# One PSUM bank told to the list scheduler, mean-attention sums ranked before weight differences, and a lead-in put in another order

## The chip, the cores and the metric

The kernel runs on one NeuronCore of a Trainium2 chip. Its engines work side by side, each through its own queue in order: TensorE (PE) multiplies matrices and transposes, VectorE (DVE), ScalarE (ACT) and GpSimd (POOL) work element by element, SyncE (SP) issues most of the DMAs. They hand work to each other by semaphores. TensorE writes to PSUM, eight banks of 2 KB in each partition; ACT and DVE read from there. The metric is the device time of one execution in microseconds (us). 0.5% of this kernel's time is 7.86 us.

## The reference

Four batches of eight heads over 576 positions with 64 channels go through two attentions, whose sum is the input of a mixture of eight experts.

```python
# mean attention: groups of 4 positions averaged, 144 x 144 softmax attention, result repeated 4 times
q_d = q.reshape(B, H, Sd, factor, D).mean(axis=3)         # k_d, v_d alike
out_up = np.repeat(sm_attn(q_d, k_d, v_d), factor, axis=2)
# local attention: each position looks at |distance| < 4, so at most 7 neighbours
mask = np.abs(pos[:, None] - pos[None, :]) < factor
...
attn_out = out_up + out_local                              # becomes x: 2304 tokens x 512
# experts
logits = x @ w_gate
P = np.exp(logits - logits.max())
for _ in range(8):                                         # Sinkhorn over all tokens and experts
    P /= P.sum(1, keepdims=True) + 1e-09
    P /= P.sum(0, keepdims=True) + 1e-09
    P *= N / E
for e in range(E):
    out += P[:, e:e+1] * (np.maximum(x @ w1[e], 0) @ w2[e])   # w1[e] 512x1024, w2[e] 1024x512
```

## The kernel before

**Products.** Every fp32 product of the experts is three passes of TensorE over rounded parts: high x high, high x low, low x high. So each weight piece is converted twice: its high half by ACT (`w1h`, `w2h`), its low half as a difference by POOL, sometimes DVE (`w1l`, `w2l`, L1994 and L1998). A unit is one 128-wide slice of one expert's hidden layer over a group of tokens: 12 matmuls give `psh` (L1842), ACT makes `hh` from it by ReLU (L1906), DVE the rest `hl` (L1909), and three matmuls for each tile of tokens (L1876 to L1878) add to `psy`.

**Stages.** (1) The lead-in computes the attention of the first 256 tokens, so that the experts can start. Its steps (`k_part`, `q_part`, `s_part`, ...) are put in order by a planner (`Plan.schedule`) from the hand-written list `LEAD` (L2138) and estimated lengths. While TensorE has nothing to do there, dummy matmuls (L2586, 128 x 400) run. (2) From then to about 560 us the units are mixed with the rest of the attention. Here generators ("threads") yield the engine they need next and the time from which they are ready, and `sched` (L2023 on) always steps the thread with the earliest estimated start, ties by `RANK` (L2019). The clocks of that estimate, one for each engine, are the program's, not the chip's: they decide only in which order instructions are written into the queues. (3) Two more plans, Mid and Final, work through the remaining tokens with a scheme that saves multiplications (`psm`, L588 to L783). The change is to stages 1 and 2.

**The bank.** One PSUM bank, `psd`, is used by several threads in turn. `d_gen` (mean attention) transposes and sums the query groups into it on TensorE (L1448), ACT copies them out as `qz` (L1457), TensorE computes scores into another bank (`pss`, L1507), later transposes the probabilities through `psd` (L1540; ACT copies out `pt`, L1545) and writes the result (L1569; ACT copies out `od`, L1578). `g_gen` (gate logits) uses it with a DVE reader. Besides, 112 columns of the same bank, `scp`, hold the weights of the local attention: DVE writes them (L1214, `psd<-sc,mx`) and reads them in four products (L1228, `prod<-lw,psd`). The framework orders any two instructions that touch the bank on different engines in the order in which they are written. The scheduler before knows two numbers of this: `psd_r`, the end of the last DVE product, for which a TensorE writer (engine name `"ped"`) waits, and `psd_w`, the end of the last TensorE write, for which a DVE product waits. ACT's copies and DVE's write of `scp` ask for neither.

**Other threads that the change touches.** `p_gen` (`"p"` in `RANK`) forms the sums for the mean attention on POOL (`dr<-lw`, `dr<-lq`, L1350). `paced` spreads DMAs for the coming part over the units. `raw_next` issues the weight pieces on SP (L1002, L1007), as buffers come free.

## Time and profile before

| | us |
|---|---|
| median of 3 runs | 1571.87 (1570.53 to 1576.81) |
| profiled execution | 1573.13 |
| its span, first to last instruction | 1571.4 |
| TensorE busy | 1555.8 |
| DVE busy | 1335.6 |
| POOL busy | 1072.3 |
| ACT busy | 823.9 |

The profiled execution took 1573.13 us, of which 1.7 us lie outside the span; it is 1.26 us above the median. TensorE is busy for 99% of the span, at a mean granted clock of 0.999 of full speed. Since a TensorE instruction counts as busy also while it is slow, single places are read from the timeline: start of one, start of the next. In a row of the timeline the part in brackets is the time for which the engine stood idle before the instruction, and what released it.

### The profile page before, as it was taken

What the parts mean: (1) busy time and instruction counts of PE and PEld (TensorE: products, weight loads), DVE (VectorE), ACT (ScalarE), POOL (GpSimd) and SP (SyncE); (2) the same over time, 40 slices, a digit from 0 to 9 for tenths busy, and PEclk for the clock granted to TensorE, in tenths of its full rate; (3) what the DMA queues carried; (4) which work ended last, traced back from release to release, by engine and by line L of the source; (5) the groups of instructions that cost most, each with busy time, mean ns of one, the idle gap of its engine ahead of it and who ended that gap; (6) DMA issues with size and microseconds to landing.
All of it is one profiled execution on the core that took longest, in us unless ns stands there. A gap on an engine that the chain in (4) does not pass through costs nothing.

```text
span 1571.4 us, 24610 instructions
## 1 busy us (share of the span) xinstructions
PE 1555.8 (99%) x8243; PEld 1315.7 (84%) x8243; DVE 1335.6 (85%) x1875; ACT 823.9 (52%) x1748; POOL 1072.3 (68%) x1022
## 2 busy tenths in 40 slices
PE   8999999999999999999999999999999999999998
PEld 7888888889887888889999988888888888888887
DVE  6778888888988696478999797999989999999987
ACT  5653555465554524365555445555555555555553
POOL 8687566769755600287777548878777777878872
PEclk9999999999999999999999999999999999999999
DMA  9877767769763645423332372212121222121102
GB/s 206 222 206 193 166 163 186 183 186 240 212 164 105 195 138 180 145 62 104 97 119 61 120 213 78 74 54 75 58 70 58 75 60 75 57 68 54 48 14 54
DMA packets 232187, 190.06 MB, mean 121 GB/s; under 512 B 28732, under 2 KB 190460, under 8 KB 232060
## 3 DMA queue, kind: packets, MB, share of 16 engines
q1 hardware_dynamic: 225068, 176.36, 41.1%
q10 hardware_dynamic: 6992, 12.13, 2.3%
q8 instruction: 64, 1.05, 0.3%
q14 instruction: 63, 0.52, 0.1%
HBM read 166.25 MB, written 22.18 MB: 120 GB/s over the span
## 4 chain that ended last, share of the span: by engine, by line
PE 83%; DMA 4%; POOL 4%; issue 4%; DVE 3%; SPq 1%; ACT 1%; ACTq 0%; POOLq 0%; DVEq 0%
PE psm L588 26%; PE psm L600 19%; PE psh L1842 14%; PE psm L783 7%; PE psy L1876 5%; PE psy L1878 4%; PE psy L1877 4%; DMA r<-in_moe_w_dram 2%; POOL w2l L1998 2%; POOL w1l L1998 2%; PE pss L1507 1%; DMA lw<-in_k_dram 1%; DVE acc L794 0%; DMA dr<-in_v_dram 0%; DMA lw<-in_v_dram 0%
## 5 line engine op out<-in xcount | busy, mean ns | idle before, releaser
L571 POOL TENSOR_TENSOR o<-r,o 128x512 fp32r<-128x512 f32 x126 | 166.0, 1317 | 88.0 <-ACT o L567 87.5
L1998 POOL TENSOR_TENSOR w1l<-r,w1h 128x512 fp32r<-128x512 f32 x114 | 155.7, 1366 | 89.4 <-ACT w1h L1975 76.9
L1998 POOL TENSOR_TENSOR w2l<-r,w2h 128x512 fp32r<-128x512 f32 x115 | 158.0, 1374 | 23.4 <-ACT w2h L1975 18.2
L588 PE MATMUL psm<-th,o 128*128 128x512 f32 x512 | 173.0, 389 | 0.0
L1876 PE MATMUL psy<-w2h,hh 128*128 128x512 f32 x408 | 165.0, 404 | 0.3 <-ACT hh L1906 0.3
L622 DVE TENSOR_TENSOR acc<-psm,acc 128x512 f32<-128x512 f32 x216 | 144.7, 682 | 20.9 <-PE psm L600 20.7
L1878 PE MATMUL psy<-w2h,hl 128*128 128x512 f32 x408 | 159.7, 391 | 0.6 <-DVE hl L1909 0.6
L1877 PE MATMUL psy<-w2l,hh 128*128 128x512 f32 x408 | 159.6, 391 | 0.0
L600 PE MATMUL psm<-hx,o 128*128 128x512 f32 x564 | 151.1, 389 | 0.0
L1906 ACT ACTIVATE hh<-psh 128x512 fp32r<-128x512 f32 (+1 forms) x136 | 67.5, 496 | 149.6 <-PE psh L1842 141.3
L571 POOL TENSOR_TENSOR o<-xh,o 128x256 fp32r<-128x256 f32 x132 | 111.2, 849 | 50.2 <-ACT o L567 42.4
L1909 DVE SCALAR_TENSOR_TENSOR hl<-psh,hh 128x512 fp32r<-128x512 f32 (+1 forms) x136 | 76.1, 561 | 69.6 <-ACT hh L1906 68.8
L588 PE MATMUL psm<-xh,o 128*128 128x512 f32 x384 | 131.2, 389 | 0.3 <-DVE hl L2094 0.3
L1842 PE MATMUL psh<-xhs,w1h 128*128 128x256 f32 (+1 forms) x384 | 125.9, 328 | 0.6 <-ACT xhs L2253 0.6
L1975 ACT ACTIVATE w2h<-r 128x512 fp32r<-128x512 f32 x134 | 84.2, 629 | 78.9 <-PE psy L1878 28.5
L600 PEld LDWEIGHTS psm<-hx,o 128*128 128x128 f32 x564 | 105.8, 188 | 22.0
L1842 PE MATMUL psh<-xls,w1h 128*128 128x256 f32 (+1 forms) x384 | 122.8, 320 | 0.5 <-DVE xls L2518 0.5
L1842 PE MATMUL psh<-xhs,w1l 128*128 128x256 f32 (+1 forms) x384 | 122.8, 320 | 0.0
L567 ACT ACTIVATE o<-r 128x512 fp32r<-128x512 f32 x139 | 87.3, 628 | 55.5 <-PE psm L600 35.6
L588 PEld LDWEIGHTS psm<-th,o 128*128 128x128 f32 x512 | 96.1, 188 | 20.1
L1252 DVE TENSOR_REDUCE lo<-prod 128x256 f32<-128x1792 f32 x32 | 109.6, 3425 | 0.1
L571 POOL TENSOR_TENSOR xh<-xh,xh 128x256 fp32r<-128x256 f32 x32 | 24.8, 782 | 116.0 <-ACT xh L567 115.8
(379 smaller groups left out, 4556.8 us busy)
## 6 DMA issues: line engine op xcount, KB each, us to landing
r<-in_moe_w_dram SPq DMA_DIRECT2D x367, 256.0 KB
xh<-in_moe_w_dram SPq DMA_DIRECT2D x108, 128.0 KB
spill<-sp ACTq DMA_DIRECT2D x40, 256.0 KB
s<-spill SPq DMA_DIRECT2D x40, 256.0 KB
xl<-in_moe_w_dram SPq DMA_DIRECT2D x68, 128.0 KB
g<-gd SPq DMA_DIRECT2D x16, 256.0 KB
sums<-dr SPq DMA_DIRECT2D x36, 64.0 KB
r2x<-in_moe_w_dram SPq DMA_DIRECT2D x9, 256.0 KB
```

What stands on the lines that cost most here:

```text
L567: self.nc.scalar.activation(out=self.get(v)["h"], in_=self.w_view(l, r, ps), func=AF.Copy)
L571: (self.nc.gpsimd if pool else self.nc.vector).tensor_tensor(out=o["l"], in0=self.w_view(l, r, ps), in1=o["h"].bitcast(F32), op=ALU.subtract)
L588: self.nc.tensor.matmul(out=ps, lhsT=wt[:, k], rhs=xt[:, k], start=start and n == 0, stop=n == 5, skip_group_check=not start,)
L600: self.nc.tensor.matmul(out=ps, lhsT=wt[:, a, 128 * m:128 * m + 128], rhs=ht, start=start and n == 0, stop=n == 5, skip_group_check=not start,
L622: self.nc.vector.tensor_tensor(out=self.get(o[0]), in0=self.get(a[0]), in1=self.get(b[0]), op=op)
L783: self.nc.tensor.matmul(out=ps, lhsT=self.at_tile(ht, t), rhs=wt[:, a], start=start and n + t % 2 == 0, stop=n == 5, skip_group_check=not ...
L1252: nc.vector.tensor_reduce(out=ot[:, :, h % 2], in_=pr.rearrange("p r w d -> p r d w"), axis=AX.X, op=ALU.add,)
L1842: nc.tensor.matmul(out=ps, lhsT=w[:, kk], rhs=x[:, kk], start=(kk == 0 and j == 0), stop=(kk == 3 and j == 2),)
L1876: nc.tensor.matmul(out=ye[z], lhsT=hh[:, ts], rhs=h2, start=(f2 == 0), stop=False)
L1877: nc.tensor.matmul(out=ye[z], lhsT=hh[:, ts], rhs=l2, start=False, stop=False)
L1878: nc.tensor.matmul(out=ye[z], lhsT=hl[:, ts], rhs=h2, start=False, stop=(f2 == NF - 1))
L1998: nc.gpsimd.tensor_tensor(out=l, in0=r, in1=h.bitcast(F32), op=ALU.subtract)
```

## The change

It has five parts.

1. **The bank in the scheduler.** Instead of `psd_r` and `psd_w` there is one time for each of TensorE, ACT and DVE (`psd_e`). Who uses the bank starts, in the estimate, no earlier than the last use by another engine. `"ped"`, `"actd"` and `"dved"` mark such steps for TensorE, ACT and DVE. The normalization of the local weights is cut in two, so that DVE can do something else between the reciprocal and the write of `scp`.
2. **Ranks and margins.** `"p"` goes from 3.5 to 2.5, which puts it before the weight differences that are not urgent (3). TensorE steps that are not units get an estimated margin of 0.4 instead of 0.15 us. The key and query windows come two parts a unit instead of one.
3. **Start of the lead-in.** 13 dummy matmuls instead of 17, and TensorE's planned start at 5.9 instead of 6.4.
4. **Its order.** `w1` (the second unit's weights) stands later in `LEAD`; its conversions wait for the first `xhs`. The mask operations of POOL (`mk...`) are planned to be due only at the end and are taken to be twice as long.
5. **The first unit.** The six matmuls of each half are sorted so that the two with `xls` come last. The clocks with which stage 2 begins are set about 1 to 2.4 us later.

```diff
-    psd_r, psd_w = [0.0], [0.0]
+    psd_e = {"pe": 0.0, "act": 0.0, "dve": 0.0}
+    def psd_after(e):
+        return max(t for z, t in psd_e.items() if z != e)
+    def on_psd(e, t):
+        psd_e[e] = t
+        return t
...
-            yield t + HOP, "dve", 0.9, True
+            yield t + HOP, "dve", 0.6, True
             nc.vector.tensor_reduce(out=mx, in_=sc3, axis=AX.X, op=ALU.add)
             nc.vector.tensor_scalar(out=mx, in0=mx, scalar1=EPS, scalar2=None, op0=ALU.add)
             nc.vector.reciprocal(out=mx, in_=mx)
+            dve(112, t)
+            dve(16, lock=True)
+            t = dve(128)
+            yield t, "dved", 0.3, True
             nc.vector.tensor_tensor(
                 out=scp.rearrange("p h r w -> p (h r) w"), in0=sc3,
...
-            dve(112, lock=True)
+            on_psd("dve", dve(112, t, psd_after("dve"), lock=True))
...
-                yield max(tv[h], psd_w[0]), "dve", 2.05, False
+                yield tv[h], "dved", 2.05, False
...
-            yield from paced(u + 1, l_win_parts(u + 1, k, l_k))
+            yield from paced(u + 1, l_win_parts(u + 1, k, l_k), 2)
...
-            t = psd_w[0] = d_done[b, hf] = pe(1.6, t0, psd_r[0])
+            t = d_done[b, hf] = on_psd("pe", pe(1.6, t0, psd_after("pe")))
             d_taken.add((b, hf))
-            yield t + HOP, "act", 0.0, False
+            yield t + HOP, "actd", 0.0, False
             for i in range(2):
                 o = slice(64 * i, 64 * i + 64)
                 nc.scalar.activation(out=qz[o, :, i, Q0:], in_=ps[o], func=AF.Copy, scale=scale / (R * R))
-                t_qk = act(2 * Q1, t)
+                t_qk = on_psd("act", act(2 * Q1, t, psd_after("act")))
...
-                for kk in part:
-                    for j, (w, x) in enumerate(((h1, vh), (h1, vl), (l1, vh))):
+                terms = [(kk, w, x) for kk in part for w, x in ((h1, vh), (h1, vl), (l1, vh))]
+                if not n:
+                    terms.sort(key=lambda z: z[2] is vl)
...
-    RANK = {"h": 0, "raw": 0, ... "p": 3.5, ... "m": 2, "v": 2}
+    RANK = {"h": 0, "raw": 0, ... "p": 2.5, ... "m": 2, "v": 2}
...
-                en = "pe" if t.eng == "ped" else t.eng
-                st = max(t.ready, clk[en])
+                en = t.eng[:-1] if t.eng in ("ped", "actd", "dved") else t.eng
+                st = max(t.ready, clk[en], psd_after(en) if en != t.eng else 0.0)
...
-                    st = max(t.ready + 0.15, clk["pe"], psd_r[0] if t.eng == "ped" else 0.0)
+                    st = max(t.ready + 0.4, st)
...
-        LEAD = "k0 q0 ... v0 t0 s2 w1 v2 ct0 ... o3 p3 x1 w0".split()
+        LEAD = "k0 q0 ... v0 t0 s2 v2 ct0 ... o3 p3 w1 x1 w0".split()
...
+            after = [x_h[0]] if n else []
...
-                op("act", f"wh{n}{j}", [v_r[n]], [a], lambda h=h, j=j: cp("act", h, r[j]), 512)
+                op("act", f"wh{n}{j}", [v_r[n]] + after, [a], lambda h=h, j=j: cp("act", h, r[j]), 512)
...
-                op("pool", f"mk{len(P.ops)}", [], [v], emit, 56)
+                op("pool", f"mk{len(P.ops)}", [], [v], emit, 120)
...
-        work = P.schedule({"act": 7.1, "dve": 5.1, "pool": 5.1, "pe": 6.4})
+        for o in P.ops:
+            if o.name.startswith("mk"):
+                o.by = P.seq[-1]
+        work = P.schedule({"act": 7.1, "dve": 5.1, "pool": 5.1, "pe": 5.9})
...
-                for _ in range(int((o.start - t - 0.1) / 0.18) if t else 17):
+                for _ in range(int((o.start - t - 0.1) / 0.18) if t else 13):
...
-        begin = {"pe": 27.0, "dve": 29.5, "act": 29.2, "pool": 29.6, "port": 29.6, "sp": 27.5, "dma": 32.0}
-        land = {"lk": 28.0, "lq": 29.0, 2: (31.0, 32.0)}
+        begin = {"pe": 28.2, "dve": 30.2, "act": 29.8, "pool": 32.0, "port": 32.0, "sp": 28.5, "dma": 33.5}
+        land = {"lk": 30.5, "lq": 33.2, 2: (34.5, 35.3)}
```

The same replacement as in `d_gen`'s first copy stands at every other use of the bank. What the new numbers do to the queues is shown at three places. The first is ACT's queue around the copy of the second half of the first batch's queries (`qz_107<-psd`), with what each instruction waits for. Before:

```order
L1578 ACTIVATE od<-psd 128x2x80 [waits PE_49]
L1975 ACTIVATE w2h<-r_1027 128x512 [waits DMAHW6_49,Pool_49]
L1906 ACTIVATE hh<-psh 128x256 [waits DVE_49,PE_49]
L1951 DMA spill<-sp 128x512 [waits Activation_49]
L1457 ACTIVATE qz_107<-psd 64x2x80 [waits DVE_49,PE_49]
L1457 ACTIVATE qz_107<-psd 64x2x80
```

After:

```order
L1585 ACTIVATE od<-psd 128x2x80 [waits PE_49]
L1984 ACTIVATE w2h<-r_1020 128x512 [waits DMAHW6_49,Pool_49]
L1915 ACTIVATE hh<-psh 128x256 [waits DVE_49,PE_49]
L1464 ACTIVATE qz_107<-psd 64x2x80 [waits PE_49]
L1464 ACTIVATE qz_107<-psd 64x2x80
```

The copy no longer waits for DVE, only for TensorE. On DVE the same place reads as follows before, where `psd<-sc,mx` and `prod<-lw,psd` are the bank's users:

```order
L1212 TENSOR_SCALAR mx<-mx 128x16
L1213 RECIPROCAL mx<-mx 128x16
L1214 TENSOR_TENSOR psd<-sc,mx 128x112
L1909 SCALAR_TENSOR_TENSOR hl<-psh,hh 128x256
L1228 TENSOR_TENSOR prod<-lw,psd 128x1792
L1514 MEMSET st 80x6
```

And after:

```order
L1220 TENSOR_SCALAR mx<-mx 128x16
L1221 RECIPROCAL mx<-mx 128x16
L1918 SCALAR_TENSOR_TENSOR hl<-psh,hh 128x256
L1226 TENSOR_TENSOR psd<-sc,mx 128x112
L1237 TENSOR_TENSOR prod<-lw,psd 128x1792
L1521 MEMSET st 80x6
```

`hl` now stands ahead of the write into the bank, which itself waits for ACT's copy. The second place is SP's queue after the lead-in: weight pieces (`r_...`), the queries of the next mean attention (`dr`) and the values of the next local window (`lw`). Before:

```order
L1002 DMA r_579<-in_moe_w_dram 128x4x128
L1007 DMA r_581<-in_moe_w_dram 128x512
L1002 DMA r_657<-in_moe_w_dram 128x4x128
L1325 DMA dr<-in_q_dram 80x4x256 x2
L1104 DMA lw<-in_v_dram 32x2x512
...
L1104 DMA lw<-in_v_dram 32x2x384
L1007 DMA r_716<-in_moe_w_dram 128x512
```

After:

```order
L1010 DMA r_575<-in_moe_w_dram 128x4x128
L1015 DMA r_577<-in_moe_w_dram 128x512
L1332 DMA dr<-in_q_dram 80x4x256 x2
L1112 DMA lw<-in_v_dram 32x2x512
...
L1112 DMA lw<-in_v_dram 32x2x384
L1010 DMA r_684<-in_moe_w_dram 128x4x128
L1015 DMA r_703<-in_moe_w_dram 128x512
```

The first weight piece of the sixth unit (`r_657` before, `r_684` after) has gone from ahead of the ten attention loads to behind them. The third place is POOL's queue at the end of the lead-in, where `dv` is the last sum of the first mean attention, `w1l` and `w2l` the first two units' weight differences and `wg` the gate's. Before:

```order
L2343 TENSOR_TENSOR dv<-vsum 72x2x2x64
L2536 TENSOR_TENSOR w1l<-r_196,w1h 128x512
L2536 TENSOR_TENSOR w2l<-r_198,w2h 128x512
L2536 TENSOR_TENSOR w1l<-r_200,w1h 128x512
L2536 TENSOR_TENSOR w2l<-r_202,w2h 128x512
L2213 TENSOR_TENSOR wg<-wgr,wg 128x4x8
L1998 TENSOR_TENSOR w1l<-r_319,w1h 128x512
```

After:

```order
L2352 TENSOR_TENSOR dv<-vsum 72x2x2x64
L2546 TENSOR_TENSOR w1l<-r_196,w1h 128x512
L2546 TENSOR_TENSOR w2l<-r_198,w2h 128x512
L2546 TENSOR_TENSOR w1l<-r_200,w1h 128x512
L2546 TENSOR_TENSOR w2l<-r_202,w2h 128x512
L2561 TENSOR_SCALAR ef<-ef 32x56
L2577 TENSOR_SCALAR mask<-ef 128x56
L2579 TENSOR_TENSOR mask<-mask 128x56
L2580 TENSOR_SCALAR mask<-mask 128x56
L2222 TENSOR_TENSOR wg<-wgr,wg 128x4x8
L2007 TENSOR_TENSOR w1l<-r_311,w1h 128x512
```

Four mask operations, which stood before the sums of the values, now stand between the weight differences and `wg`. Over the whole program two weight differences go from DVE to POOL, and four first additions to the output go through a copy by ACT; the matmuls of the units and of the attention are the same, in a slightly different mixture.

## Rows read from the trace of the kernel before

**Rows 1.** The page's line of busy times, by engine.

```profile
PE 1555.8 (99%) x8243; PEld 1315.7 (84%) x8243; DVE 1335.6 (85%) x1875; ACT 823.9 (52%) x1748; POOL 1072.3 (68%) x1022
```

**Rows 2.** The page's chain that ended last, by engine.

```profile
PE 83%; DMA 4%; POOL 4%; issue 4%; DVE 3%; SPq 1%; ACT 1%; ACTq 0%; POOLq 0%; DVEq 0%
```

**Rows 3.** Waits of TensorE: waiting line, what for, us, times, longest.

```profile
PE pss L1507 <- ACT qz L1457: 2.3, 1, 2.3
PE psg L1647 <- DVE xl L1630: 1.0, 1, 1.0
...
PE psd L1723 <- DVE stmp L1712: 0.7, 1, 0.7
```

**Rows 4.** Timeline, 66 to 72 us: start, us, instruction, [idle before].

```profile
66.33 1.33 PE L1448 MATMUL psd<-ident,dr 80*64 80x80 f32 x32
...
67.76 1.08 DVE L1214 TENSOR_TENSOR psd<-sc,mx 128x112 f32<-128x112 f32 x1 [1.22 <-PE psd L1448]
...
69.09 2.00 DVE L1228 TENSOR_TENSOR prod<-lw,psd 128x1792 f32<-128x1792 f32 x1
...
71.19 0.30 ACT L1457 ACTIVATE qz<-psd 64x160 f32<-64x160 f32 x1 [4.36 <-DVE st L1514]
...
71.54 1.08 PE L1507 MATMUL pss<-kz,qz 128*80 128x144 f32 x4 [2.27 <-ACT qz L1457]
```

**Rows 5.** Stretches: busy by engine, granted clock, DMA share, GB/s.

```profile
28.00:50.00 22.00, 20.07 (x178) 16.82 (x175) 15.69 (x16) 10.81 (x25) 14.47 (x13) 1.00 0.96 244
...
72.00:74.00 2.00, 2.00 (x11) 2.00 (x11) 0.45 (x1) 1.81 (x6) 1.46 (x2) 0.50 0.36 133
74.00:76.00 2.00, 2.00 (x10) 1.85 (x10) 0.62 (x3) 0.72 (x3) 1.05 (x1) 0.67 0.42 125
```

**Rows 6.** Timeline, 45 to 49 us: the same steps for the first half.

```profile
46.70 0.62 ACT L1457 ACTIVATE qz<-psd 64x160 f32<-64x160 f32 x2 [0.88 <-PE psd L1448]
...
48.09 0.65 PE L1507 MATMUL pss<-kz,qz 128*80 128x144 f32 x4
48.49 0.38 PE L1842 MATMUL psh<-xhs,w1h 128*128 128x256 f32 x1
```

**Rows 7.** Timeline of the lead-in, TensorE and one row of DVE.

```profile
1.33 5.95 PE L2586 MATMUL psd<-wz 128*128 128x400 f32 x17 [1.33 <-DVE wz L2131]
...
5.83 0.69 DVE L2342 TENSOR_TENSOR gs<-dr 72x512 f32<-72x512 f32 x1 [0.62 <-DMA dr<-in_k_dram]
...
7.21 1.15 PE L2249 MATMUL leadz<-ident,dr 64*64 64x64 f32 x32
8.29 1.97 PE L2249 MATMUL leady<-ident,lq 128*64 128x128 f32 x32
...
31.38 0.39 PE L1842 MATMUL psh<-xhs,w1h 128*128 128x256 f32 x1 [0.64 <-ACT xhs L2253]
32.10 0.38 PE L1842 MATMUL psh<-xls,w1h 128*128 128x256 f32 x1 [0.34 <-DVE xls L2518]
...
34.23 0.28 PE L1647 MATMUL psg<-xhs,wg 128*16 128x256 f32 x1
```

**Rows 8.** Timeline of the lead-in, POOL.

```profile
17.80 0.36 POOL L2567 TENSOR_SCALAR mask<-ef 128x56 f32<-128x56 f32 x1
...
27.58 1.28 POOL L2536 TENSOR_TENSOR w1l<-r,w1h 128x512 fp32r<-128x512 f32 x1
...
32.53 0.25 POOL L2213 TENSOR_TENSOR wg<-wgr,wg 128x32 fp32r<-128x32 f32 x1
```

**Rows 9.** Timeline of SP's queue, 33 to 45 us.

```profile
36.73 0.37 SPq L1002 DMA_DIRECT2D r<-in_moe_w_dram  x1
37.15 1.01 SPq L1325 DMA_DIRECT2D dr<-in_q_dram  x2
38.27 5.99 SPq L1104 DMA_DIRECT2D lw<-in_v_dram  x8
```

**Rows 10.** Waits of POOL: the sums of the mean attention.

```profile
POOL dr L1350 <- DMA lq<-in_q_dram: 13.9, 6, 4.0
```

More of the change, by code (lines that the diff above doesn't have):

```diff
@@ L1232, in pv_prod @@
                 if eng is nc.vector:
[L1233 to L1235 removed]
+                    return on_psd("dve", dve(R * W * D, tv[h], *deps, psd_after("dve")))
                 return pool(R * W * D, tv[h], *deps)
@@ L1276, in ld_gen @@
             yield t + HOP, "sp", 0.0, False
-            yield from paced(u + 1, l_win_parts(u + 1, k, l_k))
+            yield from paced(u + 1, l_win_parts(u + 1, k, l_k), 2)
             yield t + HOP, "sp", 0.0, False
-            yield from paced(u + 1, l_q_parts(u + 1))
+            yield from paced(u + 1, l_q_parts(u + 1), 2)
             while u not in v_free or u >= U1 and (u, 2) not in s_read:
@@ L1477, in d_gen @@
                         )
-                t = psd_w[0] = pe(0.3, t0, t1, psd_r[0])
+                t = on_psd("pe", pe(0.3, t0, t1, psd_after("pe")))
                 if p == 1:
@@ L1481, in d_gen @@
                     d_done[b, hf] = t
-                yield t + HOP, "act", 0.0, False
+                yield t + HOP, "actd", 0.0, False
                 for i in range(2):
@@ L1542, in r_gen @@
                     )
-                t2 = psd_w[0] = pe(0.1 * nb, t, psd_r[0])
-                yield t2 + HOP, "act", 0.0, False
+                t2 = on_psd("pe", pe(0.1 * nb, t, psd_after("pe")))
+                yield t2 + HOP, "actd", 0.0, False
                 nc.scalar.activation(out=pt[:, p, kh], in_=ps2.rearrange("a i t -> a (i t)"), func=AF.Copy)
-                t_pt[0] = act(nq * nb, t2)
+                t_pt[0] = on_psd("act", act(nq * nb, t2, psd_after("act")))
                 sd.free(t_pt[0])
@@ L1573, in d_gen @@
                     )
-        t = psd_w[0] = pe(8 * 0.15, t_pt[0], psd_r[0])
-        yield t + HOP, "act", 0.0, False
+        t = on_psd("pe", pe(8 * 0.15, t_pt[0], psd_after("pe")))
+        yield t + HOP, "actd", 0.0, False
         if b and hf == 0:
@@ L1580, in d_gen @@
         )
-        od_t[b, hf] = act(288, t)
+        od_t[b, hf] = on_psd("act", act(288, t, psd_after("act")))
         sd.free(od_t[b, hf])
@@ L1664, in g_gen @@
             )
-        t = psd_w[0] = pe(0.07 * nt, t, psd_r[0])
-        yield t + HOP, "dve", 0.3, False
+        t = on_psd("pe", pe(0.07 * nt, t, psd_after("pe")))
+        yield t + HOP, "dved", 0.3, False
         nc.vector.tensor_reduce(
@@ L1670, in g_gen @@
         )
-        t = dve(2 * E * nt, t)
+        t = on_psd("dve", dve(2 * E * nt, t, psd_after("dve")))
         sd.free(t)
@@ L1839, in m_gen @@
                     ps = ps_h.tile([128, nt], F32, tag="h", name="psh")
-                for kk in part:
-                    for j, (w, x) in enumerate(((h1, vh), (h1, vl), (l1, vh))):
-                        nc.tensor.matmul(
-                            out=ps, lhsT=w[:, kk], rhs=x[:, kk],
-                            start=(kk == 0 and j == 0), stop=(kk == 3 and j == 2),
-                        )
+                terms = [(kk, w, x) for kk in part for w, x in ((h1, vh), (h1, vl), (l1, vh))]
+                if not n:
+                    terms.sort(key=lambda z: z[2] is vl)
+                for z, (kk, w, x) in enumerate(terms):
+                    nc.tensor.matmul(
+                        out=ps, lhsT=w[:, kk], rhs=x[:, kk],
+                        start=(part[0] == 0 and z == 0), stop=(part[0] == 2 and z == len(terms) - 1),
+                    )
                 t = pe(mm_t(nt, 6), deps)
@@ L2047, in sched @@
                     rank = 4 if nm == "l" else 5
-                    if hq and t.eng == "dve" and t.dur > 1.0:
+                    if hq and en == "dve" and t.dur > 1.0:
                         n, _, nt, te = hq[0]
@@ L2054, in sched @@
                     rank = RANK.get(nm, 5)
-                if t.lock and t.eng == "dve" and t.dur <= 2.1 and st - max(t.ready, clk["dve"]) > PATIENCE:
+                if t.lock and en == "dve" and t.dur <= 2.1 and st - max(t.ready, clk["dve"]) > PATIENCE:
                     rank = 0.4
@@ L2266, in attention_moe_kernel @@
         v_q = there("q", 6.9)
-        v_k = [there(f"k{n}", (6.0, 9.3, 9.9, 10.8)[n]) for n in range(NP)]
+        v_k = [there(f"k{n}", (5.8, 9.3, 9.9, 10.8)[n]) for n in range(NP)]
         v_w = there("vw", 13.0)
@@ L2475, in ct_part @@
             st["pt", hf] = pt.rearrange("a (p k i t) -> a p k i t", p=2, k=2, i=2), x
-        o_at, v_s = {}, {}
+        o_at, v_s, x_h = {}, {}, {}
         def o_part(n):
@@ L2515, in x_part @@
             sx = lp.rearrange("p (z t) -> p z t", z=2)
-            xw = new(f"xh{hf}")[0]
+            xw = x_h[hf] = new(f"xh{hf}")[0]
             op("act", f"xh{hf}", [b], [xw], lambda: cp("act", xh[0][:, z, 0:256], sx), 512)
@@ L2600, in attention_moe_kernel @@
         for n in w_unit:
-            w_ready[n] = (25.7, 27.0) if n == 0 else (28.3, 29.6)
+            w_ready[n] = (27.0, 28.3) if n == 0 else (30.0, 31.3)
             raw_rel.extend(w_ready[n])
```

14 lines of the change are left out of this document (4 added, 10 removed).

## The prediction

> **What bounds the kernel now.** I read the page's busy line first: TensorE is busy for 1555.8 of 1571.4 us, the next engine, DVE, for 1335.6 [rows 1]. The chain of waits agrees: 83% of it is TensorE [rows 2]. No matmul of the units goes away, so the change can only give back time in which TensorE stood idle or ran at the lower clock, and can only lose by making it idle more. The list of TensorE's waits says how much there is: one wait of 2.3 us of the scores `pss` for ACT's copy `qz`, one of 1.0 for `xl` and one of 0.7 for `stmp`, and little else in stage 2 [rows 3]. The timeline shows what stands behind the long one [rows 4], the stretches what the clock did after it [rows 5], and the lead-in is read from its own timeline [rows 7, 8].
>
> **Part 1, the bank: the long stall.** Before, TensorE's 32 transposes into the bank end at 66.33 + 1.33 = 67.66. Then DVE takes the bank: its write of the local weights at 67.76 (1.08), one `hl`, and the product at 69.09 (2.00). ACT's copy may start only behind the product, at 71.19, after 4.36 us of idling, and `pss` starts at 71.54 after TensorE has idled 2.27 [rows 4]. In the new order ACT's copy waits for TensorE alone, and DVE's write waits for the copy. The two copies take 0.62 together where nothing comes between, as in the first half of the same queries, where `pss` followed without an idle time [rows 6]. So they run from about 67.8 to 68.4, and `pss` has its input 0.9 us before TensorE is through with its matmuls (71.54 - 2.27 = 69.27). The idle time goes: -2.3. DVE loses about 0.6 for this (its write starts at 68.4 instead of 67.76), less the `hl` that now stands ahead of it; DVE has no follower that TensorE waits for at this place, because `hl` has been moved ahead. If that cover is gone, the price is those 0.6.
>
> After the stall the granted clock is 0.50 from 72 to 74 us and 0.67 from 74 to 76, and TensorE was busy all the while [rows 5]. 0.50 is 1.2 of 2.4 GHz. Lost: 2 x 0.50 + 2 x 0.33 = 1.7 us. The stretch follows directly on the one long idle time in this stage, so with that gone I take it to go as well: -1.7. The bounds are 0 and -1.7. Part 1 together: **-4.0**.
>
> **Part 1, the other places.** The scheduler now holds an ACT copy or a DVE write back, in its estimate, while another engine has the bank, and writes other instructions ahead of it. Elsewhere in the order some copies by ACT (`pt`) now come behind a 2.0 us product of DVE that they preceded before. ACT's queue is in order, so `hh` of a unit stands behind such a copy; TensorE waits for it if the wait is longer than the other unit's matmuls last. The trace of before does not show these places. From below: each could win a stall back, but there are only the waits of 1.0 and 0.7 [rows 3], so at best -1.7 in all. From above: one bad place costs what the one in the trace did, 2.3 and the slow stretch, 4.0 [rows 3, 5]. Both waits in the list are of DVE being late at another moment than the bank's, so a reshuffled DVE queue meets them or not, about evenly: **-0.9**, with the ends -1.7 and +4.0.
>
> **Part 2, ranks and margins.** The sums on POOL (`dr`) come some units earlier, ahead of weight differences. In before they have waited 13.9 us in six places for the query loads, at most 4.0 [rows 10]. A sum in front of a difference now makes the difference wait for that load. POOL is busy for 1072 of 1571 us [rows 1], so a difference that is late by one such wait can be made up, and the wait meets TensorE only if the weights were prepared less than 4.0 ahead. I take 0, since no wait of TensorE for a difference is in the list of before [rows 3], and keep +4.0 as the end: one such wait in full. The larger margin only moves TensorE's small steps behind a unit: 0.
>
> **Parts 3 to 5, the lead-in.** 17 dummies last 5.95 us, 0.35 each, the lower level for 400 columns [rows 7]. Four fewer free TensorE 1.4 us earlier, at about 5.85. The first keys are there: DVE's first sum of them starts at 5.83, released by their DMA [rows 7]. So the first transposes start at 5.85 instead of 7.21, -1.36, unless they now run at the lower level: 32 of them take 1.15 at full speed [rows 7], at most twice that, so they end between 1.36 and 0.2 earlier. What follows is a chain over four engines, and POOL's part is relieved too, as the four mask operations (0.36 for the one shown [rows 8], some 1.6 in all) leave its path ahead of the values' sums. The first unit idles 0.64 and 0.34 for its second `xhs` and `xls` [rows 7]; sorted, it meets the second of these later, -0.3. Gain at the second unit: 1.7 at best.
>
> Part of it is lost again within 15 us. First, the mask operations now stand ahead of `wg`. POOL's four differences take from 27.58 to 32.53 [rows 8], 4.95 us; begun 1.5 us earlier, plus 1.6 for the masks, `wg` is done at about 32.9, and the gate's matmuls, at 34.23 before [rows 7], would want it at 32.5: +0.5. Second, the sixth unit's first weights. Before, SP issued them at 36.73, then the queries from 37.15 and the values from 38.27 for 5.99 us [rows 9]. Now they come behind all ten loads, of 1.54 MB. SP no longer waits until 36.73, so the loads start at about 33.7. With two pieces in flight, the loads and the piece itself, 2.3 MB at the 244 GB/s of this stage [rows 5] take 9.4 us: landing at 43.1 at the earliest, and up to 47 if more is in flight. The sixth unit started at 48.49 [rows 6] and now wants its weights at about 47, after a conversion and a difference that take 1.3 more. So the loss lies between 0 and 1.3, I take +0.5. The lead-in nets -1.7 + 0.5 + 0.5 = **-0.7**, with the ends -1.7 and, if the first transposes run slowly and both losses come in full, +1.0.
>
> The moment at which the clock rises could itself move. The Trainium skill ("TensorE: Matmul & The Clock Gate", Part 1, "What's actually happening") says that the default state is the throttled one and that activity releases it. In the trace the dummies ran at the lower level up to about 7 us and the first transposes at full speed, so row and rule agree on the order. The same page says that the moment varies from run to run, by half a microsecond; by that rule the -1.36 would be -1.36 plus or minus 0.5, which no row here can show.
>
> **The sum.** -4.0 - 0.9 - 0.7 = -5.6 us against the profiled execution: 1573.13 - 5.6 = 1567.5. That execution lies 1.26 above the median of the runs. Against the median the forecast is 1571.87 - 5.6 = **1566.3**. A change of 0.5%, 7.86 us, is about what a measurement of this kernel can tell from none: faster means below 1564.0, slower above 1579.7.
>
> **Rivals.**
>
> *A: everything goes.* The stall, its slow stretch, both other waits and the whole gain of the lead-in: -4.0 - 1.7 - 1.7 = -7.4, 1564.5. For it: a scheduler that knows the bank can avoid several short waits at once, and small idle times that I left out may go too, which would bring it below 1564.0. Against it: the late weights and `wg`.
>
> *B: the stall moves.* It goes at 71 us, but one of the new places, where ACT's `pt` stands behind a product of 2.0, costs the same: +4.0 - 4.0, with the lead-in -0.7 and none of the -0.9: 1571.2. For it: DVE's product still holds the bank for 2.00 us each time [rows 4], and only the order was changed. Against it: the estimate that sets the order counts this very thing.
>
> *C: slower.* The mechanism is ACT's queue: the copy out of the bank is written behind a DVE product, the product starts late on the chip because DVE's queue lags behind the estimate, ACT stands still with `hh` behind it, TensorE idles over 2 us and its clock falls. One such place costs 4.0 [rows 3, 5]; with the -5.6 it needs two to be slower at all and four to be seen: 1571.87 - 5.6 + 4 x 4.0 = 1582.3. Against it: DVE, at 85%, has room, and in before, where nothing told the scheduler of the bank on ACT, this happened once.
>
> *D: the clock rises later.* With fewer dummies the lower level lasts through the first transposes and the queries' ones: 1.15 + 1.97 more [rows 7], less the 1.4. That is +1.7 in place of the -0.7: 1568.7.
>
> **How the numbers follow.** Forecast 0.50 (own range 1563.5 to 1569), A 0.16, B 0.15, C 0.10, D 0.09. Faster by over 0.5%: A's lower part, 0.11, and the forecast's tail below 1564.0, 0.11, together 0.22. Slower by over 0.5%: C, of which some stops short, but with lesser mishaps of the same kind beside it: 0.09. Within: the rest, 0.69. The range for 8 in 10 takes in A and D, and B with two places of half the price: 1560.5 to 1574.
>
> **What would show it.** Right: in the list of TensorE's waits no `pss` behind `qz` over 0.5; ACT's `qz` of the second half starting within 0.2 us of the end of the transposes; the granted clock at 1.00 all through stage 2. The first transposes start at 5.9 and the second unit 1 to 1.7 earlier than before. `psg` waits for `wg` on POOL about 0.5 and a `psh` at about 47 for a weight conversion or its DMA. Wrong: a wait of TensorE over 1.5 us for `hh` or `hl` between 40 and 560 us, with ACT at `pt`, `od` or `qz` behind DVE's `prod` at that moment; a stretch with a granted clock of 0.5 there; or first transposes that take over 2 us.

## The result and the profile after

The changed kernel takes 1588.77 us (median of 4 runs, 1588.63 to 1591.61), the kernel before 1571.2 beside it: ratio 1.011, 95% interval 1.0082 to 1.0137. It is 17.6 us slower. Forecast were 1566.3, a change within 0.5%, and a range up to 1574. The prediction was wrong in sign and size.

The page's busy line and chain of the changed kernel, against [rows 1, 2]:

```profile
PE 1562.4 (98%) x8239; PEld 1320.0 (83%) x8239; DVE 1328.2 (84%) x1873; ACT 827.6 (52%) x1752; POOL 1076.5 (68%) x1024
...
PE 78%; DMA 8%; DVE 5%; POOL 3%; issue 3%; SPq 2%; ACT 1%; ACTq 0%; POOLq 0%; DVEq 0%
```

The span grew from 1571.4 to 1589.8, by 18.4. TensorE's busy time rose by 6.6 although four dummies are gone: the same matmuls ran longer at the lower clock (mean granted clock 0.994, before 0.999). The rest is new idle time. The chain shows where it is from: DMA has doubled its share, TensorE has lost 5 points. The waits of TensorE, answering to [rows 3]:

```profile
PE psh L1851 <- POOL w1l L2007: 5.8, 4, 3.5
PE psd L1480 <- DMA dq<-sums: 4.5, 5, 1.8
PE psd L1576 <- DMA dv<-sums: 2.5, 1, 2.5
PE psg L1654 <- POOL wg L2222: 1.3, 1, 1.3
...
PE psh L1851 <- ACT w1h L1984: 1.3, 1, 1.3
```

Here `dq` and `dv` are the queries and values of the mean attention, which go as sums from POOL through DRAM (`sums`) and are read back by DMA. The wait of 2.3 for `qz` is gone, and 12.8 us of waits for weight differences (`w1l`) and for the mean attention's sums (`dq`, `dv`) have come, which the kernel before did not have. To see when, I take in both traces the start of the unit matmul that has the same number of matmul columns of units ahead of it (below: by equal columns):

| place in stage 2 (time before) | 29.3 | 53 | 79 | 149 | 160 | 284 | 301 | 379 | 445 | 494 | 583 |
|---|---|---|---|---|---|---|---|---|---|---|---|
| after minus before, us | -2.0 | +0.6 | -3.8 | -2.2 | +3.4 | +2.5 | +9.4 | +14.0 | +10.8 | +19.9 | +17.8 |

The gains that were forecast are in it: -2.0 at the first unit, and -4.3 between 59 and 79 us for the bank. But from 149 us on there are large losses, with smaller gains between them. From 605 us on, at +18.6, nothing changes any more. The place of the old stall, against [rows 4]:

```profile
66.86 1.33 PE L1455 MATMUL psd<-ident,dr 80*64 80x80 f32 x32
...
68.23 0.62 ACT L1464 ACTIVATE qz<-psd 64x160 f32<-64x160 f32 x2 [0.89 <-PE psd L1455]
68.89 0.28 DVE L1226 TENSOR_TENSOR psd<-sc,mx 128x112 f32<-128x112 f32 x1 [1.08 <-ACT qz L1464]
69.26 2.02 DVE L1237 TENSOR_TENSOR prod<-lw,psd 128x1792 f32<-128x1792 f32 x1
69.63 0.65 PE L1514 MATMUL pss<-kz,qz 128*80 128x144 f32 x4
```

Copy, write, product, and `pss` without an idle time: as predicted. The lead-in, against [rows 7]:

```profile
1.33 4.70 PE L2599 MATMUL psd<-wz 128*128 128x400 f32 x13 [1.33 <-DVE wz L2140]
5.96 1.49 PE L2258 MATMUL leadz<-ident,dr 64*64 64x64 f32 x32
...
27.30 0.39 PE L1851 MATMUL psh<-xhs,w1h 128*128 128x256 f32 x1
...
33.33 0.29 PE L1654 MATMUL psg<-xhs,wg 128*16 128x256 f32 x1 [1.34 <-POOL wg L2222]
...
47.83 0.63 ACT L1984 ACTIVATE w1h<-r 128x512 fp32r<-128x512 f32 x1 [4.11 <-DMA r<-in_moe_w_dram]
...
48.51 0.39 PE L1851 MATMUL psh<-xhs,w1h 128*128 128x256 f32 x1 [1.26 <-ACT w1h L1984]
```

The first transposes take 1.49, partly at the lower level; the first unit is 2.0 early and the second 2.4 (30.41 against 32.80); `wg` and the sixth unit's weights take back 1.34 and 1.26, each more than the 0.5 that I had taken.

Now two of the new places, from the timeline. First POOL and TensorE around 290 us:

```profile
280.59 2.97 SPq L1112 DMA_DIRECT2D lw<-in_v_dram  x8
...
283.93 0.64 ACT L1984 ACTIVATE w1h<-r 128x512 fp32r<-128x512 f32 x1
...
289.12 3.20 POOL L1357 TENSOR_TENSOR dr<-lw 128x256 f32<-128x256 f32 x2 [4.75 <-DMA r<-in_moe_w_dram]
292.28 1.26 POOL L2007 TENSOR_TENSOR w1l<-r,w1h 128x512 fp32r<-128x512 f32 x1
...
293.60 0.79 PE L1851 MATMUL psh<-xhs,w1l 128*128 128x512 f32 x1 [3.49 <-POOL w1l L2007]
```

POOL stands still for 4.75 us at a sum `dr` of a window (`lw`). The profile names a weight DMA as what ended the wait; the sum itself reads only the window, whose eight loads SP issued from 280.59 to 283.6, so I take the window for what was missing. The difference `w1l`, whose high half ACT had formed at 283.93, stands behind it in the queue, and TensorE waits 3.49 for it. The second place is the queries of the second batch, at 149 us:

```profile
145.19 0.81 SPq L1410 DMA_DIRECT2D dq<-sums  x2
...
148.59 0.25 PE L1480 MATMUL psd<-ident,dq 72*128 72x72 f32 x1 [0.60 <-DMA dq<-sums]
149.79 0.28 PE L1480 MATMUL psd<-ident,dq 72*128 72x72 f32 x1 [0.94 <-DMA dq<-sums]
150.00 0.69 PE L1885 MATMUL psy<-w2h,hh 128*128 128x512 f32 x1
```

Here TensorE's transposes stand in its queue before their data are there, and the units behind them wait too. After both places the clock falls, against the stretch of [rows 5]:

```profile
150.00:152.00 2.00, 2.00 (x8) 1.63 (x7) 1.13 (x1) 1.38 (x4) 0.29 (x1) 0.52 0.75 251
152.00:154.00 2.00, 2.00 (x7) 1.54 (x7) 0.00 (x0) 0.63 (x1) 1.37 (x2) 0.62 0.00 0
...
292.00:294.00 2.00, 0.41 (x1) 0.41 (x2) 0.00 (x0) 0.00 (x0) 2.00 (x3) 0.86 0.00 0
294.00:296.00 2.00, 2.00 (x6) 1.52 (x6) 0.00 (x0) 0.00 (x0) 2.00 (x3) 0.50 0.55 146
296.00:298.00 2.00, 2.00 (x9) 1.57 (x8) 0.00 (x0) 0.28 (x1) 2.00 (x3) 0.78 0.68 181
```

There are two more such places, TensorE's rows and the stretches:

```profile
467.11 0.25 PE L1480 MATMUL psd<-ident,dq 72*128 72x72 f32 x1 [1.76 <-DMA dq<-sums]
505.18 1.23 PE L1576 MATMUL psd<-pt,dv 72*64 72x144 f32 x8 [2.49 <-DMA dv<-sums]
...
467.00:471.00 4.00, 3.69 (x11) 2.97 (x12) 1.86 (x1) 0.92 (x4) 0.55 (x1) 0.57 0.69 218
505.00:509.00 4.00, 3.83 (x21) 2.92 (x22) 2.42 (x2) 0.93 (x2) 2.11 (x2) 0.51 0.69 194
509.00:513.00 4.00, 4.00 (x15) 3.30 (x14) 1.55 (x3) 1.12 (x2) 1.82 (x2) 0.64 0.23 68
```

At the lower clock 1.7 us are lost at each of the first three places and 3.4 at the last (4 x 0.49 + 4 x 0.36). With the waits themselves the four cost 1.5 + 1.7, 3.5 + 1.7, 1.8 + 1.7 and 2.5 + 3.4, together 17.8 us, as much as the kernel lost. The smaller new waits (1.34, 1.26, 1.17, 1.02 and shorter ones, some 7 us) and what was gained (4.0 and 2.0) nearly cancel.

### The profile page after: what moved, and what is told of

Its sections match the earlier page's. It is cut to its first block, busy times and chain, and to the rows that moved or that the text cites. A ratio compares the mean times of both kernels' runs of the same rounds, so it can differ in the third digit from the quotient of the medians.

```text
span 1589.8 us, 24612 instructions
## 1 busy us (share of the span) xinstructions
PE 1562.4 (98%) x8239; PEld 1320.0 (83%) x8239; DVE 1328.2 (84%) x1873; ACT 827.6 (52%) x1752; POOL 1076.5 (68%) x1024
## 4 chain that ended last, share of the span: by engine, by line
PE 78%; DMA 8%; DVE 5%; POOL 3%; issue 3%; SPq 2%; ACT 1%; ACTq 0%; POOLq 0%; DVEq 0%
PE psm L588 26%; PE psm L600 19%; PE psh L1851 12%; PE psm L783 6%; PE psy L1885 4%; PE psy L1887 4%; PE psy L1886 4%; DMA r<-in_moe_w_dram 2%; DMA lw<-in_k_dram 2%; DVE prod L1170 1%; DMA lw<-in_v_dram 1%; DMA lq<-in_q_dram 1%; POOL dr L1357 1%; POOL w1l L2007 1%; DVE prod L1237 1%
## 5 line engine op out<-in xcount | busy, mean ns | idle before, releaser
L571 POOL TENSOR_TENSOR o<-xl,o 128x256 fp32r<-128x256 f32 x92 | 79.1, 865 | 33.3 <-ACT o L567 26.9
```

The costliest lines, as they stand in the source:

```text
L571: (self.nc.gpsimd if pool else self.nc.vector).tensor_tensor(out=o["l"], in0=self.w_view(l, r, ps), in1=o["h"].bitcast(F32), op=ALU.subtract)
```

## The experiments

**First round: which part of the change does it?** Theory R held the rank of the sums (2.5 before weight differences) for the cause, rival K the bank, rival C of this round (not the C of the prediction) the starting clocks of stage 2. The larger margin and the faster pacing of part 2 were not run apart.

*rank_undone*, the changed kernel with one number back:

```diff
-"p": 2.5
+"p": 3.5
```

> The changed kernel with the rank of the mean-attention sums back at 3.5, nothing else. Theory R (rank): the sums, written ahead of weight differences on POOL, wait there for window loads, so w1l comes late, and because the order takes the sums for early, TensorE's transposes of dq and dv are written before their data can be there. Then both kinds of wait go (w1l 5.8 us, dq 4.5, dv 2.5, and the slow stretches behind them), the long stall of before stays away, and the time is 1567 to 1573. Rival K (bank): the new order of the bank's users is what writes TensorE's transposes too early. Then only the waits for w1l go with their slow stretches, about 8 us: 1580 or more.

Measured: 1597.18, ratio 1.0169 (1.0150 to 1.0189), slower still. Its longest waits of TensorE:

```profile
PE psd L1576 <- DMA dv<-sums: 6.8, 2, 5.0
PE psx L1619 <- DVE xl L1637: 3.8, 1, 3.8
PE psd L1480 <- DMA dq<-sums: 3.7, 2, 3.4
```

No wait for `w1l` is left among them, but `dv` and `dq` are later than ever. Theory R falls in this form. The timeline of POOL shows the other side of the same coin, around 400 us:

```profile
398.62 1.30 POOL L2007 TENSOR_TENSOR w2l<-r,w2h 128x512 fp32r<-128x512 f32 x1
399.88 0.75 POOL L1361 TENSOR_TENSOR dr<-dr 128x256 f32<-128x256 f32 x1
```

With the old rank a sum stands behind weight differences. Its store and the read of `dv` follow on SP, and TensorE waits 4.96 for that `dv` at 411.43.

*rank_only*, the kernel before with `"p": 2.5`:

> The kernel before with the rank of the sums at 2.5, nothing else. Theory R: the losses of stage 2 appear without the rest of the change, 12 to 22 us above before: 1583 to 1593, with waits for w1l and for dq or dv in TensorE's list and the 2.3 us wait for qz still there or somewhere else. Rival K: only the waits for w1l, so at most 8 us: 1571 to 1579.

Measured: 1591.33, ratio 1.0125 (1.0109 to 1.0141). The total is in R's range, and the waits that R names are all there: 3.9 for `dq`, 1.9 for `dv`, 2.3 for `qz`, though only 1.0 for `w1l`. Beside them stand 3.1 and 2.4 for DVE on the bank, which R does not name. So the rank by itself can cost 20 us, and taking it back out of the changed kernel cost more still: neither value of it is the cause alone. A number that fits is no proof.

*bank_only*, the kernel before with `psd_e`, the split step and `"actd"`, `"dved"`, and the old margin:

```diff
-                    st = max(t.ready + 0.15, clk["pe"], psd_r[0] if t.eng == "ped" else 0.0)
+                    st = max(t.ready + 0.15, st)
```

> The kernel before with the bank's times in the scheduler alone (old rank, old margin of 0.15, old lead-in, old pacing). Theory R: the wait for qz and its slow stretch go, 4.0 us less, and little is lost: 1565 to 1569. Rival K: waits for dq or dv of 5 to 12 us with their slow stretches: 1576 to 1583.

Measured: 1582.64, ratio 1.007 (1.0047 to 1.0094), K's total, but not its waits of 5 to 12: for `dq` only 2.4, and 2.8 for `xhs`, 2.0 for `hx` and 1.4 for `xls`. The old stall is gone (-4.3 between 59 and 79 us, by equal columns), and more is lost elsewhere, 9 us of it between 246 and 259.

*lead_only*, the kernel before with parts 3 to 5 of the change:

> The kernel before with the lead-in alone (13 dummies, new order, sorted first unit, new starting clocks). Theory R and rival K alike: the first unit starts 2.0 us earlier, as in the changed kernel (27.30 instead of 29.30), and by the fourth unit of the stream 2.6 are lost again, so +0.6 or less; stage 2 as before: 1570 to 1573. Rival C (clocks): the starting clocks of stage 2, set 1 to 2.4 us later, are what shifts the order for the worse; then 5 us or more are lost in stage 2: above 1576.

Measured: 1579.85, ratio 1.0048 (1.0030 to 1.0066): rival C's range. At 59 us it is 1.2 us ahead, at 301 us 0.6 behind, at 605 us 2.8 behind, and it loses 4.7 more where the next stage starts, far from the lead-in. So each of the three parts that were run by itself loses, and in different places. That gave theory S: what loses is not the work of any part but the order of stage 2, which the scheduler deals anew whenever one of its estimates changes.

**Second round: parts with the order held, and the order without parts.**

*lead_old_clocks* has the changed lead-in and the old starting clocks. All queues of stage 2 are then those of before.

```diff
-        begin = {"pe": 28.2, "dve": 30.2, "act": 29.8, "pool": 32.0, "port": 32.0, "sp": 28.5, "dma": 33.5}
+        begin = {"pe": 27.0, "dve": 29.5, "act": 29.2, "pool": 29.6, "port": 29.6, "sp": 27.5, "dma": 32.0}
```

> The kernel before with the changed lead-in (13 dummies, new order, sorted first unit) but the old starting clocks of stage 2, so that every queue of stage 2 is written in the order of before. Theory S (the order is dealt anew): what the change loses in stage 2 comes from no part of its own; any change of the program's estimates makes the scheduler pick otherwise, and the order of before was one that happened to fit the chip. Then here stage 2 is as in before and only the lead-in's own effect is left: 2 us earlier at the first unit, part of it lost at wg, so -2 to 0: 1569 to 1572. Rival L (the lead-in itself harms): its new moments at the start set off the later waits; then 1577 to 1581, as with the lead-in alone.

Measured: 1571.47 against 1571.88, ratio 0.9999 (0.9990 to 1.0009). The lead-in harms nothing, and gives nothing that can be measured: by equal columns it is 1.9 ahead at the first unit and 1.9 behind at 53 us, with waits of 1.3 for `wg` and 1.6 for an `hh` behind it, which a slow stretch follows. The stall for `qz` is here too, and it shows that a slow stretch need not follow one:

```profile
73.43 0.80 PE L1507 MATMUL pss<-kz,qz 128*80 128x144 f32 x4 [2.28 <-ACT qz L1457]
...
74.00:78.00 4.00, 4.00 (x30) 3.70 (x29) 2.61 (x5) 3.85 (x11) 3.02 (x3) 1.00 0.40 135
```

*swap_one* is the kernel before with the pending copy (`pend` holds ACT's copies of `qz` that are still to be written) written ahead of DVE's write of the local weights; the estimates are untouched.

```diff
+            for f in list(pend):
+                copy_out(f)
             nc.vector.tensor_tensor(
                 out=scp.rearrange("p h r w -> p (h r) w"), in0=sc3,
```

> The kernel before with one thing moved and all estimates left as they were: where ACT's copy qz is pending when DVE writes the local weights into the bank, the copy is written first. Only ACT's queue changes, by one place. Theory S: the stall of 2.3 us and the slow stretch behind it go and nothing else changes, -4.0: 1566 to 1569. Rival K (knowing the bank is itself what harms): DVE's write and product, late by 0.6, make other waits, and the gain is under 2: 1570 or more.

Measured: 1568.86 against 1571.88, ratio 0.9975 (0.9967 to 0.9984): -3.9 us by the ratio, -3.0 between the medians. The wait for `qz` is not in TensorE's list, and the stretch behind it stays at the full clock:

```profile
72.00:74.00 2.00, 2.00 (x17) 1.89 (x16) 2.00 (x1) 1.98 (x6) 1.02 (x1) 1.00 0.77 194
```

This is the -4.0 of the prediction, alone. Against the trace of before the distance goes from -1.2 at 66 us, where nothing has been changed yet, to -5.2 at 79 us, and stays between -4.2 and -5.3 down to 600 us.

*swap_and_lead*, both:

> Both of the former together. Theory S: the gains add up, -4 to -6: 1565 to 1568, below before and the changed kernel. Rivals L and K: above 1572.

Measured: 1567.83, ratio 0.9975 (0.9965 to 0.9984). Faster than either kernel, and within S's range, but only by the swap: the lead-in adds nothing that can be measured.

*clocks_only* is the opposite: the kernel before, lead-in and all, with only the starting times that the change gives the scheduler: its `begin` and `land` lines and the times of the first two units' weights (`w_ready`). The clocks are 0.6 to 2.4 us later, the landings up to 4.2.

> The kernel before with nothing changed but the numbers with which the scheduler's clocks start stage 2 (28.2 instead of 27.0 for TensorE and so on); the lead-in is that of before. Theory S: the order is dealt anew, and without any part of the change's own work the time rises by 5 us or more, with waits of TensorE of the same kinds (dq or dv for their DMA, psd for another engine): 1577 to 1592. Against S: within 3 us of before.

Measured: 1583.04, ratio 1.0069 (1.0051 to 1.0086). No work of the change is in it, only another order, and 11 us are lost. Two of its waits:

```profile
PE psm L588 <- DVE hx L757: 3.0, 1, 3.0
PE psd L1473 <- DMA dq<-sums: 2.3, 3, 1.7
```

The order is another all through stage 2: in the order of the two traces some 870 of 8243 matmuls stand elsewhere. The old stall at 71 us went away here too (-4.4 between 59 and 79 us), though nothing in this kernel tells the scheduler of ACT's part in the bank. The wait of 3.0, 0.7 before, is a second kind of loss: it stands where the Mid plan starts. Mid's first weights (L550) are issued by SP 17 us later than in before, behind reloads (`s`) and copies (`xc`) that the new order has left over; 3 of the 17 are the lag that it brings along. SP's rows of before and of clocks_only:

```profile
637.98 4.51 SPq L550 DMA_DIRECT2D xh<-in_moe_w_dram  x8
```

```profile
651.94 0.42 SPq L2685 DMA_DIRECT2D xc<-xl  x1
655.22 3.97 SPq L550 DMA_DIRECT2D xh<-in_moe_w_dram  x8
```

That `hx` is late because of these weights is argued from SP's rows, not tried. By equal columns, 3.1 of the loss lie before 605 us and 4.4 at this place. lead_only and the two nudges below have the same wait of 3.0.

**Third round: how small a nudge, and what is wrong with the new orders?** *nudge_dma* and *nudge_dve* each change one number of the kernel before:

```diff
-"sp": 27.5, "dma": 32.0}
+"sp": 27.5, "dma": 32.5}
```

> The kernel before with one number changed: the scheduler's DMA clock at the start of stage 2 is 32.5 instead of 32.0. Nothing of the work changes. Theory S: this deals the order of stage 2 anew; the time rises by 5 us or more, with the wait for qz gone or kept as it falls and new waits for dq, dv or another engine on the bank: 1577 to 1592. Against S (it needs a real change of the lead-in or of a rank): within 3 us of before, 1569 to 1575.

> The kernel before with one number changed: the scheduler's DVE clock at the start of stage 2 is 29.8 instead of 29.5. Theory S: another deal, other places, again 5 us or more: 1577 to 1592. Against S: 1569 to 1575.

Measured: 1579.64, ratio 1.0041 (1.0028 to 1.0054), and 1582.89, ratio 1.0071 (1.0051 to 1.0091). Half a microsecond in an estimate costs 6.7, 0.3 in another 10. Theory S holds: the order alone can lose. Where it loses here is in the larger part the start of Mid: by equal columns nudge_dma is 0.8 ahead of before at 605 us and loses 3.1 there, nudge_dve is 3.1 behind and loses 4.4. And the same program varies with the clock: the two executions of nudge_dma at a mean granted clock of 1.000 took 1575.45 and 1576.05, the three at 0.995 to 0.997 took 1579.64 to 1581.48.

But S does not say why a fresh order (a new deal) is worse rather than better. Theory O: the estimate takes the mean-attention data for earlier than they are, so a fresh deal writes what waits for them too early. *both_later* is the changed kernel with two later estimates:

```diff
-            yield t0 + HOP, "pool", 1.3, True
+            yield t0 + 4.0, "pool", 1.3, True
...
-                d_sum[b, hf, s] = (t, t_in)
+                d_sum[b, hf, s] = (t, t_in + 3.0)
```

> The changed kernel whose scheduler takes the mean-attention data for later: 4.0 us instead of 0.06 after the window's estimated landing for POOL's sums, and 3 us later for dq, dk and dv. Theory O (the new orders lose because the estimate has these data too early): TensorE's waits for w1l (5.8), dq (4.5) and dv (2.5) fall to under 2 together, and with the slow stretches behind them 12 us or more come back: 1566 to 1577. Theory S alone (a fresh deal, good or bad by chance, whatever its estimates): no better on average than the changed kernel, other waits in their place: 1580 to 1595.

Measured: 1571.1 against 1572.93, ratio 0.9986 (0.9977 to 0.9995); the changed kernel had 1.011. Some 19 us come back. In its list of waits there is none for `dq` or `dv`, and 0.3 and 0.2 are left for `w1l`. And POOL, whose waits at the sums in the changed kernel and in this one stand here one after the other, stands for 10.8 us in front of windows instead of 51.0:

```profile
POOL dr L1357 <- DMA lq<-in_q_dram: 15.4, 7, 6.7
POOL dr L1357 <- DMA r<-in_moe_w_dram: 14.3, 4, 6.1
POOL dr L1357 <- DMA lw<-in_k_dram: 12.3, 3, 5.0
POOL dr L1357 <- DMA lw<-in_v_dram: 9.0, 3, 4.3
```

```profile
POOL dr L1357 <- DMA lq<-in_q_dram: 6.8, 3, 3.5
...
POOL dr L1357 <- DMA lw<-in_v_dram: 4.0, 2, 3.0
```

*swap_lead_wg* is swap_and_lead with the gate's low half on DVE:

```diff
-            nc.gpsimd.tensor_tensor(
+            nc.vector.tensor_tensor(
                 out=wg[:, :, E:2 * E], in0=wgr, in1=wg[:, :, 0:E].bitcast(F32), op=ALU.subtract
```

> The order of before held, with the one copy moved and the changed lead-in, and besides the gate's low half formed by DVE, which is idle there, instead of by POOL behind the mask operations. The wait of 1.0 us for wg goes; where the lead-in gave 0 so far it gives 1: 1565.5 to 1568, the fastest of all. If something else is late by as much, 1567 to 1569.

Measured: 1569.6, ratio 0.9979 (0.9970 to 0.9988), above both expected ranges and no better than without. The wait for `wg` is gone, and one of 1.7 for `hh` has taken its place.

**Fourth round: a cure or a lucky deal?** Three losing deals and the changed kernel got the later estimates (*sums_later* the second only).

> The kernel before with DVE's starting clock at 29.8, as in the run nudge_dve (ratio 1.0071), and besides both later estimates of the run both_later. Theory O: no wait of TensorE for dq or dv over 0.5 is left (2.7 in three places before) and the time falls by 5 us or more against nudge_dve: 1568 to 1577. Theory S alone: as likely above as below nudge_dve, 1575 to 1592.

> The run clocks_only (ratio 1.0069; waits for dq 2.3 and dv 1.4) with both later estimates. Theory O: those waits gone, 1568 to 1577. Theory S alone: 1575 to 1592.

> The run rank_undone, the slowest of all (ratio 1.0169; waits for dv 6.8, xl 3.8, dq 3.7), with both later estimates. Theory O: the waits for dv and dq go with their slow stretches, 15 us or more: 1567 to 1582. Theory S alone: 1575 to 1597.

> The changed kernel with only the second of the later estimates, 3 us for dq, dk and dv; POOL's sums keep their early time and stand ahead of weight differences. Theory O: the waits for dq (4.5) and dv (2.5) go with their slow stretches, those for w1l (5.8) stay: about 8 to 12 us below the changed kernel, 1576 to 1581. Theory S alone: any of 1570 to 1595.

| deal | ratio as it was | with later estimates |
|---|---|---|
| nudge_dve | 1.0071 (1.0051 to 1.0091) | 1.0027 (1.0018 to 1.0037) |
| clocks_only | 1.0069 (1.0051 to 1.0086) | 1.0021 (1.0010 to 1.0031) |
| rank_undone | 1.0169 (1.0150 to 1.0189) | 1.0019 (1.0009 to 1.0030) |
| changed, second estimate only | 1.0110 (1.0082 to 1.0137) | 1.0026 (1.0016 to 1.0036) |
| changed, both | the same | 0.9986 (0.9977 to 0.9995) |

All five fall, the first three to nearly one level (1576.73, 1576.72 and 1575.87; *sums_later* 1577.04). These times lie in O's ranges, but in S's too, so the totals of single runs do not decide. Two other things speak for O. The eight fresh orders with the early estimates lie 0.4 to 1.7% above before, the five with later ones between -0.14 and +0.27%: no order of the one group lies among the other, though the intervals of the two nearest (1.0028 to 1.0054 and 1.0018 to 1.0037) overlap. And no wait of TensorE for the DMA of `dq` or `dv` is left in the first three; in *sums_later* `dq` is down from 4.5 to 0.6. One expectation failed: in *sums_later* the waits for `w1l` should have stayed at 5.8, but 1.7 remain, though POOL's sums have their early time there. So what the first estimate does by itself is not shown. By equal columns, in the profiled executions, one sees where each came back:

| us behind the trace of before | as it was: at 605 us, at the end | with later estimates: at 605 us, at the end |
|---|---|---|
| changed, both | 18.6, 18.5 | -1.7, -1.7 |
| changed, second estimate only | 18.6, 18.5 | 3.3, 7.0 |
| rank_undone | 23.4, 23.5 | 3.4, 3.4 |
| nudge_dve | 3.1, 7.5 | 1.8, 1.8 |
| clocks_only | 3.1, 7.5 | 4.2, 4.3 |

For the changed kernel and rank_undone it is stage 2, as O says. For nudge_dve and clocks_only it is mostly the start of Mid, where the wait for `hx` is back at 0.7. That is no wait for mean-attention data: the later estimates also gave an order in which Mid's weights come in time, and *sums_later*, with one of the two, has 2.4 there. In stage 2 clocks_only gained nothing, because another wait came, which was 0.7 long in [rows 3] and costs 5.5 by equal columns between 547 and 550 us, as it does in nudge_dve (5.6). It is more than these two still lie behind. *clocks_only_later*:

```profile
PE psd L1723 <- DVE stmp L1712: 3.8, 1, 3.8
PE psh L1842 <- DVE xls L1630: 1.9, 1, 1.9
```

## Why the prediction was wrong

**The step that failed** is "Part 1, the other places", with part 2 beside it. It took stage 2 for the order of before with some local moves, and priced it as -0.9 with ends of -1.7 and +4.0, "one bad place". In fact the order of the whole stage was dealt anew, from any one of the change's numbers, and the new deal had four bad places of 3 to 6 us each. The ends should have been those of a fresh order, not of a known order with one fault. clocks_only, nudge_dma and nudge_dve show it without any of the change's work: +6.7 to +11.

**Part 2, rank and POOL's sums.** The mechanism was named (a difference waits behind a sum that waits for its window) and set to 0 because no such wait stood in the list of before. It came: 5.8 us in four places, the longest with the slow stretch of 294 to 298. The reason given was void: the list of before shows what the old order avoids, not what a new one will. And [rows 10] is only the first line of several: in before POOL stood at such sums for 38.1 us in 13 places, up to 5.5 at a time, and in the changed kernel for 51.0 in 17, up to 6.7, so the 4.0 was too short an end as well. But the rank as such is not the cause, since undoing it made things worse.

**Part 1, the bank.** Right, and in size: -4.0 forecast, -3.9 by the ratio and -3.0 between the medians with the order held. The wait of 2.3 goes; that the slow stretch of 1.7 went with it in full is in part luck of the trace, since in lead_old_clocks the same wait of 2.28 is followed by a clock of 1.00. That the scheduler has to know the bank for this is not shown: the stall also vanished in clocks_only.

**Parts 3 to 5, the lead-in.** The second unit came 2.4 earlier, 1.7 was called the best. In part that is the one trace of before, whose first unit is the latest of nine traces with the old lead-in (28.66 to 29.30; with the new one 27.18 to 27.68): on the average of nine and nine the first unit gains 1.5 and the second 2.1. The two losses were named and mis-sized: 0.5 each, measured 1.34 and 1.26 (+0.22 for the difference of the same weights). Of the net -0.7 the held order shows -0.2, between -1.6 and +1.4, so it neither bears it out nor excludes it.

**The rivals.** C had the side, four places, and a time below the measured one (1582.3). Its price of 4.0 for a place with its slow stretch was of the right size; the four cost 3.2 to 5.9. Its mechanism, ACT's copy behind a product with `hh` behind it, is not what happened; the waits are for `w1l`, `dq` and `dv`. Its chance of 0.10 was argued from the single stall in before, the same mistake as above. D did not happen: the first transposes took 1.49, not over 2. But the moment at which the clock rises does move, by more than the half microsecond that the prediction gave it, and traces can show it. With the same 13 dummies the first transposes, 1.15 long at full speed, read in rank_undone and in rank_undone_later as follows; in the second the dummies too ended earlier, after 4.01 us instead of 4.70:

```profile
5.96 1.79 PE L2258 MATMUL leadz<-ident,dr 64*64 64x64 f32 x32
```

```profile
5.27 1.15 PE L2258 MATMUL leadz<-ident,dr 64*64 64x64 f32 x32
```

**The clock.** Of the 18.4 us some 7 are slow stretches: 8.5 at the four places, 1.7 in before. I had used this in the price of one place, and it held at these four. It did not hold at the waits of 0.6 to 1.3 that no slow stretch followed, nor always at longer ones (2.28 in lead_old_clocks, 3.00 in nudge_dma).

**What stays open.** Of what the later estimates gave back, the part at the start of Mid was not tried apart from the part for `dq` and `dv`. No run made some other estimate later by as much, so it is not shown that it must be this one. The order of before with the later estimates was not run either. That nudge_dve and clocks_only with later estimates still stand 0.2 to 0.3% above before is put down to the wait for `stmp` from the traces; no run took it away. Nor was the bank's model tried by itself with the later estimates, so what it is worth over the one swapped copy is not known.

## What to carry to other kernels

Where a list scheduler writes the queues, an edit of its estimates is not a local edit: hold the order and measure the part, and hold the part and measure a fresh order, before either is priced. The waits that a trace does not show are those that its order avoids, so they are no bound for another order; look instead at what the estimate takes for earlier than the trace has it. Make the estimate honest about late DMA data first: the five orders made that way here came within 0.3% of the tuned one, the eight others lay 0.4 to 1.7% above it.

## What was not expected

A change of 0.3 us in one starting clock of the program, which moves no work, cost 10 us of 1572. And TensorE, idle for 1.5 to 3.5 us at four places of the changed kernel, ran the next 4 us and more at a granted clock of 0.50 to 0.78, with its queue full: each of the waits at 149 and 293 us cost 1.7 more than its own length (2 x 0.48 + 2 x 0.38, and 2 x 0.14 + 2 x 0.50 + 2 x 0.22). Yet it is not certain: the same wait for `qz` was followed by a slow stretch in before (2.27) and by none in lead_old_clocks (2.28), and executions of one program differ by that.
